# Second MoE's w_out by Strassen's algorithm, its output transposed, with the cosine's rounding on ScalarE and a pool for late weight conversions

## The chip, the cores and the metric

The kernel runs on one core of a Trainium2 chip. The metric is the device time of one execution, in microseconds (us). Times are medians of several runs, and beside them stands one execution taken by the hardware profiler. The engines are PE (TensorE, matrix products), DVE (VectorE), ACT (ScalarE), POOL (GpSimd) and SP (SyncE, which here only issues DMAs). PSUM holds matmul results in eight banks, SBUF the other tiles, DRAM the tensors.

## The reference

Block-causal attention (4 batches, 8 heads, 576 positions, head size 64) is followed by two mixtures on the 2304 tokens of 512 features. The change touches the second one alone.

```
def _moe_ref(x, w1, w2, w3, w_out):
    h = np.maximum(np.maximum(x @ w1, x @ w2), x @ w3)      # 512 -> 768
    return (h @ w_out).astype(np.float32)                   # 768 -> 512

def _moe2_ref(x, w_in, w_out):
    h = x @ w_in                                            # 512 -> 2048
    g = h * np.cos(h)
    return (g @ w_out).astype(np.float32)                   # 2048 -> 512
```

## The kernel before

**A recorded plan.** The program is not issued as it is written. Every operation is recorded with its dependencies (class `Plan`), priced by a table, and list-scheduled in several passes (`forward`, `backward`, `run`); the best order found is issued, in program order on each engine, with semaphores between engines. All instructions therefore carry line 214, and groups are told apart by tile names. `R.copy` and `R.scale` may go to ACT or DVE, as the plan chooses.

**Products in three parts.** A float32 product is made of three matmuls on operands split into a high and a low part (`split`: a rounding copy `hi`, then `lo = t - hi` on DVE): high x high, high x low, low x high.

**Stages.** Attention runs first, with matmuls of the first MoE put between its steps (`fill`, `units`). Weights arrive as 64-bit words and are converted on ACT and DVE (`whole`: two scalings, then three DVE operations), split, and kept in SBUF (first MoE) or stored to DRAM (`kept`, second MoE). `AHEAD` lists such conversions; eight of its eleven entries are called during attention (`ahead`, from the 17th item on), the others while the first MoE finishes. The first MoE leaves its result y, transposed, in DRAM in five parts (`y_dram`).

**Second MoE, first product.** The 2304 tokens make three superblocks of 768 (`NS`), each two halves of `TK` = 384 columns. In each there are eight steps j (`HALF`), and step j makes the rows j and j + 8 of h (128 features each) for both halves by Strassen's algorithm: seven products instead of eight on blocks of 256 x 128 and 256 x 384, each in two parts of K and three matmuls, that is 42 matmuls of 384 columns (`hstage`). The seven combinations of weights come ready from DRAM (`load_pair`: three tiles of 512 KB and one of 256 KB per step), those of y are made and split once per superblock (`split_y`, 14 operands). Three PSUM banks A, Bk, C collect the products, and DVE and ACT add them up into the tiles `ha`, `hu`, `hv`, `hh`.

**Cosine.** Each of the four tiles is scaled and rounded to an integer on DVE, reduced by 2 pi on DVE, put through Sin on ACT, multiplied on DVE and split into `gh` and `gl`. This is four times per step, on 384 columns.

**Second MoE, second product.** `ostage` of step j runs one step behind (`LAG`). Six PSUM banks hold 768 tokens x 512 features of the output; for each 128 tokens and each of the two rows of g, three matmuls with g as the stationary and w_out as the moving operand of 512 columns are added to the bank: 36 matmuls per step. After the eighth step the banks are copied to `osb` and stored. Half of w_out's tiles stay in SBUF, the others are loaded again; 13 of the 16 are converted in the second MoE's first superblock (`load_out`).

**Pools.** Pools open and close in the plan too: `wc`, where most tiles of the second MoE lie, opens when the first MoE's weights and work tiles are given up (`moe`, `wk`); `wb` opens when attention's pool closes.

Of the kernel before, what the change touches and what calls it, by code (L numbers as in the profile page):

```python
# [467 lines left out]
def fused_kernel(tc, qk, qk4, q1, k1, v2, w1, w2, w3, wout, w_in2, w_out2, out):  # L468
# [58 lines left out]
    def whole(src, pool, bufs):  # L527
# [4 lines left out]
        t = cv.tile([P, 512], F32, "t", tag="t", bufs=4)  # L532
# [371 lines left out]
    CVR = 2  # L904

# [14 lines left out]
    def pair_sums(j):  # L920

        x, y = (whole(w_in2[fc], cv, CVR) for fc in (j, j + HALF))
        a, b = (cv.tile([P, 512], F32, "t", tag="t", bufs=4) for _ in range(2))
        one, two = slice(0, QUARTER), slice(QUARTER, 2 * QUARTER)
        R.vector.tensor_tensor(a[:, one], y[:, one], y[:, two], ALU.add)
        R.vector.tensor_tensor(a[:, two], a[:, one], x[:, one], ALU.subtract)
        R.vector.tensor_tensor(b[:, one], x[:, one], y[:, one], ALU.subtract)
        R.vector.tensor_tensor(b[:, two], x[:, two], a[:, two], ALU.subtract)
        return x, a, b, y[:, two]

    def keep_pair(j):
        for n, t in enumerate(pair_sums(j)):
            both = cv.tile([P, 2, 512], F32R, "both", tag="raw", bufs=CVR)[:, :, :t.n]
            split(both[:, 0], both[:, 1], t)
            kept["in", j, n] = dram.tile([P, 2, t.n], F32, f"kept_in{j}_{n}")
            R.sync.dma_start(kept["in", j, n], f32(both))

    def keep_out(fc):
        both = cv.tile([P, 2, 512], F32R, "both", tag="raw", bufs=CVR)
        convert(w_out2[:, fc], both[:, 0], both[:, 1], cv, CVR)  # L940
        kept["out", fc] = dram.tile([P, 2, 512], F32, f"kept_out{fc}")
        R.sync.dma_start(kept["out", fc], f32(both))
# [5 lines left out]
    def ahead():  # L948
        if AHEAD and converted[0] == 4 * NFF:
            AHEAD.pop(0)()  # L950

# [30 lines left out]
    for n in range(NI + 1):  # L982
# [23 lines left out]
        if n > 16 and n % 3 and len(AHEAD) > 3:  # L1006
            ahead()
# [6 lines left out]
    wb = R.open(at, name="wb", bufs=1, side="right")  # L1014
    ps_o = R.open(ps_x, name="ps_o", bufs=1, space=PSUM, side="right")
    GROUPS = (512, 512, 512, QUARTER)

    def load_pair(n):

        where = {}  # L1020
        for x, w in enumerate(GROUPS):
            if n == 0 and x == 3:
                continue
            pool, bufs = (wc, 3) if x == 3 else (wb, 1) if n % 3 == 0 else (wc, 2)
            t = pool.tile([P, 2, w], F32R, f"pair{x}", tag=f"pair{x}", bufs=bufs)
            R.sync.dma_start(f32(t), kept["in", n % HALF, x])
            where[x] = t
        return where

    NY, FIXED = 18, 14  # L1030
    y_count = [0]

    def y_tile():
        slot = y_count[0] % NY
        y_count[0] += 1
        return (wb if slot < FIXED else wc).tile([P, 2, TK], F32R, f"y{slot}", tag=f"y{slot}")
# [5 lines left out]
    def split_y(s):  # L1042

        parts7 = [[y_tile() for k in range(2)] for _ in range(7)]
        for k in range(2):
            r = {}
            for i in range(2):
                for x in range(2):
                    r[i, x] = wb.tile([P, TK], F32, "yr", tag="yr", bufs=4)
                    load_y(r[i, x], k + 2 * i, 2 * TK * s + TK * x, TK)  # L1050
            a, b = (wb.tile([P, TK], F32, f"sum{i}", tag=f"sum{i}", bufs=1) for i in range(2))

            def put(n, t):
                split(parts7[n][k][:, 0], parts7[n][k][:, 1], t)

            sub = [ALU.subtract]
            put(0, r[0, 0])
            R.vector.tensor_tensor(a, r[0, 1], r[0, 0], *sub)
            R.vector.tensor_tensor(b, r[1, 1], a, *sub)
            put(1, b)  # L1060
            put(2, r[1, 0])
            R.vector.tensor_tensor(r[0, 1], r[1, 1], r[0, 1], *sub)
            put(3, r[0, 1])
            put(4, a)
            R.vector.tensor_tensor(r[1, 0], r[1, 0], b, *sub)
            put(5, r[1, 0])
            put(6, r[1, 1])
        return [[[parts7[n][k][:, i] for k in range(2)] for i in range(2)] for n in range(7)]

    ys = {0: split_y(0)}  # L1070
    pairs = {0: None}
    while AHEAD or fill:
        if AHEAD:
            ahead()
            if 0 in pairs and pairs[0] is None and ("in", 0, 3) in kept:
                pairs[0] = load_pair(0)
        for _ in range(2):
            if fill:
                fill.pop(0)[1]()
    R.close(wk)  # L1080
    R.close(moe, wk)

    wc = R.open(moe, name="wc", bufs=1)
    TWO_PI = 2.0 * math.pi
    woh, wol, g, banks = {}, {}, {}, {}

    def load_out(s, j):

        stays = j % 2 == 0
        if stays and s:  # L1090
            return
        for fc in (j, j + HALF):
            slot = f"out{fc}" if stays else f"out{j % 4}_{fc // HALF}"
            w = wc.tile([P, 2, 512], F32R, slot, tag=slot)
            if ("out", fc) in kept:
                R.sync.dma_start(f32(w), kept["out", fc])
            else:
# [156 lines left out]
```

## Time and profile before

| | us |
|---|---|
| median of 3 runs (846.71 to 847.55) | 846.73 |
| the profiled execution | 846.43 |
| its span, first to last instruction | 844.7 |
| PE busy | 835.3 (99%) |
| PE weight loads (beside matmuls) | 723.5 (86%) |
| DVE busy | 636.3 (75%) |
| ACT busy | 486.0 (58%) |
| POOL busy | 5.5 (1%) |

Busy time of an engine is the time in which at least one of its instructions ran. Matmuls are pipelined, so that each lasts longer than the distance from its start to the next one's start; what a matmul costs in a full stream is that distance. The same holds for DVE, whose instructions overlap a little. The stretches of the profile show the engines stage by stage, the chain of waits what ended last, the timelines single instructions. DMAs of all stages moved 155.15 MB, a mean of 184 GB/s.

### The profile page before, as it was taken

How to read it: one execution, taken by the hardware profiler on the slowest of the kernel's cores; microseconds unless marked ns; L12 is line 12 of the kernel's file. 1: busy time of each engine (PE TensorE's matmuls, PEld its weight loads, DVE VectorE, ACT ScalarE, POOL GpSimd, SP SyncE). 2: the span in 40 equal slices, each digit the busy share in tenths (PEclk: the TensorE clock that was granted, in tenths of full speed). 3: DMA queues.
4: the chain of work that ended last, by engine and by line, in shares of the span. 5: the costliest groups of instructions: out<-in, count | busy, mean ns of one | idle time of the engine just before them, and what ended most of it. 6: DMA issues, size and time to landing. Idle time of an engine off the chain costs nothing.

```text
span 844.7 us, 13582 instructions
## 1 busy us (share of the span) xinstructions
PE 835.3 (99%) x4722; PEld 723.5 (86%) x4722; DVE 636.3 (75%) x1441; ACT 486.0 (58%) x1114; POOL 5.5 (1%) x38
## 2 busy tenths in 40 slices
PE   8999999999999999999999999999999999999998
PEld 6787888888888888888899899899899899899896
DVE  7999999678877789536645899989746778757563
ACT  7998999658867678423333564645423445433333
POOL 2000000000000000000000000000000000000000
PEclk9999999999999999999999999999999999999999
DMA  8765665675566656442354857634866146935301
GB/s 287 224 191 158 205 203 178 193 222 177 179 210 220 193 185 224 142 149 106 131 167 153 343 177 245 234 137 149 310 230 215 48 152 209 335 105 185 100 1 75
DMA packets 68627, 155.15 MB, mean 184 GB/s; under 512 B 8528, under 2 KB 26960, under 8 KB 68560
## 3 DMA queue, kind: packets, MB, share of 16 engines
q1 hardware_dynamic: 68560, 154.30, 54.8%
q8 instruction: 37, 0.61, 0.3%
q14 instruction: 30, 0.25, 0.1%
HBM read 122.29 MB, written 31.98 MB: 183 GB/s over the span
## 4 chain that ended last, share of the span: by engine, by line
PE 95%; DVE 2%; ACT 2%; DMA 0%; issue 0%; POOL 0%; ACTq 0%; POOLq 0%
PE psm L214 56%; PE po L214 23%; PE tb L214 6%; PE X L214 4%; PE SB L214 3%; PE SA L214 3%; DVE top L214 1%; ACT other L214 0%; ACT prob L214 0%; DVE t L214 0%; DMA y<-hm 0%; ACT pt L214 0%; DVE pt L214 0%; DVE prob L214 0%; DVE other L214 0%
## 5 line engine op out<-in xcount | busy, mean ns | idle before, releaser
L214 PE MATMUL psm<-y,pair 128*128 128x384 f32 x1008 | 192.4, 337 | 1.6 <-ACT ha L214 1.4
L214 PEld LDWEIGHTS psm<-y,pair 128*128 128x128 f32 x1008 | 179.0, 188 | 10.7 <-ACT ha L214 1.8
L214 PE MATMUL po<-out,gh 128*128 128x512 f32 x576 | 178.5, 391 | 0.0
L214 PE MATMUL psm<-xhi,whi 128*128 128x512 f32 (+1 forms) x360 | 136.7, 380 | 0.7 <-ACT hm L214 0.7
L214 PE MATMUL psm<-xhi,wlo 128*128 128x512 f32 (+1 forms) x360 | 133.0, 370 | 0.0
L214 PE MATMUL psm<-xlo,whi 128*128 128x512 f32 (+1 forms) x360 | 132.9, 369 | 0.0
L214 PEld LDWEIGHTS po<-out,gh 128*128 128x128 f32 x576 | 106.9, 188 | 16.1
L214 PE MATMUL po<-out,gl 128*128 128x512 f32 x288 | 113.1, 393 | 0.0
L214 ACT ACTIVATE th<-th,halfpi 128x384 f32<-128x384 f32 x96 | 58.6, 617 | 72.4 <-DVE th L214 72.0
L214 PEld LDWEIGHTS psm<-xhi,wlo 128*128 128x128 f32 x360 | 67.9, 189 | 11.8
L214 PEld LDWEIGHTS psm<-xhi,whi 128*128 128x128 f32 x360 | 67.9, 189 | 9.6 <-ACT hm L214 1.0
L214 PEld LDWEIGHTS psm<-xlo,whi 128*128 128x128 f32 x360 | 68.1, 189 | 8.5
L214 DVE TENSOR_TENSOR hm<-psm,hm 128x512 f32<-128x512 f32 (+1 forms) x60 | 38.1, 635 | 47.8 <-PE psm L214 40.3
L214 ACT COPY pt<-tb 128x512 f32<-128x512 f32 (+2 forms) x100 | 58.4, 605 | 15.3 <-PE tb L214 15.0
L214 PEld LDWEIGHTS po<-out,gl 128*128 128x128 f32 x288 | 54.0, 187 | 11.5
L214 ACT CAST gh<-th 128x384 fp32r<-128x384 f32 x94 | 47.4, 510 | 27.6 <-DVE th L214 26.9
L214 DVE TENSOR_TENSOR hu<-psm,ha 128x384 f32<-128x384 f32 x24 | 13.4, 557 | 57.3 <-PE psm L214 47.8
L214 PE MATMUL tb<-ident,prob 128*128 128x128 f32 x374 | 54.7, 274 | 1.5 <-ACT pt L214 0.9
L214 PEld LDWEIGHTS tb<-ident,prob 128*128 128x128 f32 x374 | 45.0, 140 | 11.6 <-issue 2.2
L214 DVE TENSOR_TENSOR gl<-th,gh 128x384 fp32r<-128x384 f32 x96 | 51.9, 553 | 2.2 <-ACT gh L214 1.2
L214 ACT COPY hm<-psm 128x512 f32<-128x512 f32 (+1 forms) x48 | 26.0, 546 | 39.3 <-PE psm L214 33.4
L214 PE MATMUL psm<-hh,vhi 128*128 128x512 f32 (+1 forms) x120 | 46.0, 383 | 0.0
(152 smaller groups left out, 1448.3 us busy)
## 6 DMA issues: line engine op xcount, KB each, us to landing
pair<-kept_in SPq DMA_DIRECT2D x72, 512.0 KB, 5.3
kept_in<-both SPq DMA_DIRECT2D x24, 512.0 KB, 3.2
out<-kept_out SPq DMA_DIRECT2D x19, 512.0 KB, 6.2
raw<-w SPq DMA_DIRECT2D x18, 512.0 KB, 4.1
raw<-w_out SPq DMA_DIRECT2D x16, 512.0 KB, 3.6
raw<-w_in SPq DMA_DIRECT2D x16, 512.0 KB, 4.1
k<-k SPq DMA_DIRECT2D x24, 288.0 KB, 3.1
pair<-kept_in SPq DMA_DIRECT2D x24, 256.0 KB, 6.5
```

What stands on the lines that cost most here:

```text
L214: return lambda: getattr(real, method)(*[value(a) for a in args], **{k: value(a) for k, a in kw.items()})
```

## The change

**w_out by Strassen's algorithm.** The second product now takes the same form as the first, with the output transposed: w_out's combinations are stationary, and operands made of g are moving, 384 columns wide. Per superblock `ostage` runs once, behind all eight steps of `hstage`. It goes through the seven products in the order 1, 2, 6, 7, 4, 5, 3; for each and for each j it makes one operand of g (product 6 needs three differences of tiles of g first, product 7 one), splits it, and issues two units (d) of three matmuls. Four pairs of banks are used; products 1 and 2, 7 and 4, 5 and 3 add into the same bank, which is read in between. The output is written as (512, 2304); the transposition back happens outside of the kernel.

**Cosine.** The results of a step lie in one tile `g{j}` of four parts (h, v, a, u), and the chain runs on two parts at once, 768 columns: rounding on ACT, reduction on DVE, Sin on ACT, product on DVE, in place. There is no split here any more; `ostage` makes it.

**Conversions.** All 16 conversions of the second MoE go by pairs (`keep_pair`): eight of w_in, eight of w_out, each with four sums of 256 columns and four splits. Eight (w_in) are called in attention, five while the first MoE finishes, in a pool of their own (`cx`, with 6 raw and 12 spare tiles), three in the first superblock's steps.

**Buffers.** Weights of both products go through one ring of 14 slots of 512 KB (`w_tile`, 4 of them in `wb`), loaded in the order of use and reloaded for every superblock. Moving operands go through one ring of 22 (`operand`, 8 of them in `wb`), for y and for g. `bank8` takes the eight PSUM banks in turn.

```diff
-        t = cv.tile([P, 512], F32, "t", tag="t", bufs=4)
+        t = pool.tile([P, 512], F32, "t", tag="t", bufs=spare)
...
-    AHEAD = [lambda fc=fc: keep_out(fc) for fc in (9, 11, 13)]
-    for j in range(HALF):
-        AHEAD.insert(2 * j + 1 if j < 3 else len(AHEAD), lambda j=j: keep_pair(j))
+    AHEAD = [lambda *room, k=k, j=j: keep_pair(k, j, *room) for k in ("in", "out") for j in range(HALF)]
...
-        if n > 16 and n % 3 and len(AHEAD) > 3:
+        if n > 16 and n % 3 and len(AHEAD) > LEFT:
             ahead()
...
+    NW, NY, W_FIXED, Y_FIXED = 14, 22, 4, 8
...
+    def w_tile(shape):
+        slot = w_count[0] % NW
+        w_count[0] += 1
+        return (wb if slot < W_FIXED else wc).tile([P] + shape, F32R, f"w{slot}", tag=f"w{slot}")
...
+    ORDER = (1, 2, 6, 7, 4, 5, 3)
+    loads = []
+    for s in range(NS):
+        for j in range(HALF):
+            loads += [(s, "in", j, 0), (s, "in", j, 1)] + [(s, "last", j // 2)] * (j % 2 == 0) + [(s, "in", j, 2)]
+        loads += [(s, "out", n, q) for n in ORDER for q in range(HALF // 2)]
...
-        for f, x, t in ((j, 0, h), (j + HALF, 1, v), (j + HALF, 0, a), (j, 1, u)):
-            c = wc.tile([P, TK], F32, "th", tag="th", bufs=4)
...
-            R.vector.tensor_scalar(i32(c), t, 1.0 / TWO_PI, 0.25, ALU.mult, ALU.add)
+        for x in (0, 2):
+            t = both[:, x:x + 2].rearrange("p x t -> p (x t)")
+            c = wc.tile([P, 2 * TK], F32, "c", tag="c", bufs=2)
+            R.scalar.activation(i32(c), t, AF.Copy, scale=1.0 / TWO_PI, bias=0.25)
             R.vector.scalar_tensor_tensor(c, i32(c), -TWO_PI, t, ALU.mult, ALU.add)
             R.scalar.activation(c, c, AF.Sin, bias=halfpi)
-            R.vector.tensor_tensor(c, t, c, ALU.mult)
-            split(gh, gl, c)
-            g[s, f, x] = (gh, gl)
+            R.vector.tensor_tensor(t, t, c, ALU.mult)
+        g[j] = h, u, a, v
...
-    def ostage(s, j):
-        for x in range(2):
-            for t in range(TK // P):
...
-                for f in (j, j + HALF):
-                    gh, gl = g[s, f, x]
-                    with R.unit():
-                        for i, (a, w) in enumerate([(gh, woh[f]), (gh, wol[f]), (gl, woh[f])]):
-                            R.tensor.matmul(banks[n], a[:, ts], w, start=(f == 0 and i == 0),
-                                            stop=(f == NFC - 1 and i == 2))
...
+    def ostage(s):
...
+        for n in ORDER:
+            for j in range(HALF):
+                h, u, a, v = g[j]
+                if n == 6:
+                    R.vector.tensor_tensor(h, u, h, sub)
+                    t2 = wc.tile([P, TK], F32, "e", tag="e", bufs=4)
+                    R.vector.tensor_tensor(t2, v, h, sub)
+                    R.vector.tensor_tensor(a, a, t2, sub)
+                if n == 7:
+                    R.vector.tensor_tensor(u, v, u, sub)
+                y = operand()
+                split(y[:, 0], y[:, 1], {1: h, 2: a, 6: None, 7: u, 4: a, 5: h, 3: v}[n] or t2)
+                for d in range(2):
...
+                    three(ps[key], w, y, n in (1, 6, 7, 5) and j == 0, j == HALF - 1)
+                load_weights(len(loaded) + (j % 2))
...
+    for s in range(NS):
+        for j in range(HALF):
+            ahead()
+            load_weights(len(loaded) + 4)
             hstage(s, j)
...
+        ostage(s)
+        if s + 1 < NS:
+            ys[s + 1] = split_y(s + 1)
```

**How the order moves.** Three places follow, each of the kernel before and then of the changed one.

The first is DVE at the entry to the second MoE, of the kernel before, from the first step's first addition on. Here `hu`, `hv`, `ha`, `hh` are the step's sums, `th` the cosine's tile, `t`, `raw` and `out0`, `out8` belong to conversions of w_out.

```order
L214 TENSOR_TENSOR hu_5619<-psm_5585,ha_5608 128x384
L214 TENSOR_TENSOR out0_5612<-t_5357,out0_5612 128x512
L214 TENSOR_TENSOR out8_5621<-t_5510,out8_5621 128x512
L214 TENSOR_SCALAR th_5645<-hh_5636 128x384
L214 TENSOR_TENSOR hv_5653<-psm_5585,ha_5608 128x384
L214 SCALAR_TENSOR_TENSOR th_5645<-th_5645,hh_5636 128x384
L214 TENSOR_SCALAR t_5643<-t_5643 128x512
L214 TENSOR_TENSOR hv_5653<-psm_5647,hv_5653 128x384
```

In the changed kernel `g0` is the first step's tile, `hm` the first MoE's last output, `y8` to `y13` are operands of y whose tiles lie in `wc`, and `t`, `raw` belong to the one pair of w_out that is converted here.

```order
L214 COPY hm_5838<-psm_5784 128x256
L214 TENSOR_SCALAR t_5858<-raw_5793 128x512
L214 COPY g0_5860<-psm_5850 128x384
L214 TENSOR_SCALAR t_5858<-t_5858 128x512
L214 TENSOR_TENSOR g0_5860<-psm_5834,g0_5860 128x384
L214 SCALAR_TENSOR_TENSOR t_5858<-raw_5793,t_5858 128x512
L214 TENSOR_SCALAR t_5879<-raw_5816 128x512
L214 ISA t_5858<-raw_5793,t_5858 128x1024
L214 TENSOR_TENSOR y8_5877<-sum0_5582,y8_5877 128x384
L214 TENSOR_TENSOR y9_5889<-sum0_5678,y9_5889 128x384
L214 TENSOR_TENSOR y10_5894<-yr_5498,y10_5894 128x384
L214 TENSOR_TENSOR g0_5860<-psm_5834,g0_5860 128x384
```

The splits of y8 to y13 now stand between the evictions of the first step; before, all 14 were made ahead of it.

The second place is PE inside a step of the middle superblock of the kernel before; `pair` are w_in's weights, `po` the output banks.

```order
L214 MATMUL psm_7903<-y16_6386,pair1_7681 128x384 x3
L214 MATMUL psm_7903<-y17_6832,pair1_7681 128x384 x3
L214 MATMUL psm_7888<-y0_6690,pair0_7659 128x384 x3
L214 MATMUL psm_7888<-y1_6811,pair0_7659 128x384 x3
L214 MATMUL po_7046<-out6_6392,gh_7806 128x512 x2
L214 MATMUL po_7046<-out6_6392,gl_7815 128x512
L214 MATMUL psm_7903<-y2_6708,pair2_7716 128x384 x3
L214 MATMUL psm_7903<-y3_6835,pair2_7716 128x384 x3
```

The changed kernel's PE in the middle superblock's w_out: psm_7752 and psm_7761 are the banks of products 1 and 2, psm_7876 and psm_7885 those of 6, psm_7994 and psm_8000 those of 7, `w7` to `w13` weight slots.

```order
L214 MATMUL psm_7752<-y10_7818,w7_7683 128x384 x3
L214 MATMUL psm_7752<-y11_7896,w7_7683 128x384 x3
L214 MATMUL psm_7761<-y10_7818,w7_7683 128x384 x3
L214 MATMUL psm_7761<-y11_7896,w7_7683 128x384 x3
L214 MATMUL psm_7876<-y13_7881,w8_7675 128x384 x3
L214 MATMUL psm_7885<-y13_7881,w8_7675 128x384 x3
L214 MATMUL psm_7994<-y20_7812,w12_7759 128x384 x3
L214 MATMUL psm_8000<-y20_7812,w12_7759 128x384 x3
L214 MATMUL psm_7994<-y21_7839,w12_7759 128x384 x3
L214 MATMUL psm_8000<-y21_7839,w12_7759 128x384 x3
L214 MATMUL psm_7994<-y0_7847,w13_7795 128x384 x3
```

Matmuls of w_out no longer lie between those of w_in's steps; they follow each other, with products 6 and 7 interleaved.

The third place is DVE in a step of w_in, before at the end of the middle superblock's steps; `sum0`, `yr` and `y2`, `y4` belong to the next superblock's y.

```order
L214 TENSOR_SCALAR th_7937<-hh_7929 128x384
L214 SCALAR_TENSOR_TENSOR th_7937<-th_7937,hh_7929 128x384
L214 TENSOR_TENSOR hv_7950<-psm_7903,ha_7900 128x384
L214 TENSOR_TENSOR y2_7944<-yr_7759,y2_7944 128x384
L214 TENSOR_TENSOR th_7937<-hh_7929,th_7937 128x384
L214 TENSOR_TENSOR hv_7950<-psm_7946,hv_7950 128x384
L214 TENSOR_TENSOR y4_7958<-yr_7667,y4_7958 128x384
L214 TENSOR_TENSOR gl_7976<-th_7937,gh_7970 128x384
L214 TENSOR_TENSOR ha_7900<-psm_7903,ha_7900 128x384
L214 TENSOR_TENSOR sum0_7989<-yr_7931,yr_7785 128x384
```

The changed kernel's DVE in the middle superblock, around steps 4 and 5: `y0_7593` is an operand of w_out's product 1, and `g3_7386<-g3_7386` are differences that products 6 and 7 need.

```order
L214 TENSOR_TENSOR g5_7538<-psm_7529,g5_7538 128x384
L214 SCALAR_TENSOR_TENSOR c_7544<-c_7544,g4_7460 128x768
L214 TENSOR_TENSOR g4_7460<-psm_7456,g4_7460 128x384
L214 TENSOR_TENSOR g4_7460<-psm_7497,g4_7460 128x384
L214 TENSOR_TENSOR g3_7386<-g3_7386 128x384
L214 TENSOR_TENSOR g5_7538<-psm_7529,g5_7538 128x384
L214 TENSOR_TENSOR g4_7460<-g4_7460,c_7544 128x768
L214 SCALAR_TENSOR_TENSOR c_7576<-c_7576,g4_7460 128x768
L214 TENSOR_TENSOR g5_7538<-psm_7579,g5_7538 128x384
L214 TENSOR_TENSOR y0_7593<-g4_7460,y0_7593 128x384
L214 TENSOR_TENSOR g3_7386<-g3_7386 128x384
L214 TENSOR_TENSOR g4_7460<-g4_7460,c_7576 128x768
```

The rounding (TENSOR_SCALAR) and the split's subtraction (`gl`) have left the step; in their place stand differences and operands for w_out's products, made ahead of them.

## Rows read from the trace of the kernel before

**Rows 1.** The page of the profile, its first line.

```profile
span 844.7 us, 13582 instructions
```

**Rows 2.** Stretches: start:end, length, busy us (instructions) by engine, clock, DMA share, GB/s.

```profile
100.00:353.00 253.00, 253.00 (x1639) 210.56 (x1639) 211.04 (x468) 192.32 (x473) 0.00 (x0) 1.00 0.61 195
353.00:466.00 113.00, 112.78 (x641) 99.37 (x637) 54.11 (x110) 36.63 (x76) 0.00 (x0) 1.00 0.41 138
466.00:591.00 125.00, 123.57 (x623) 112.30 (x624) 116.00 (x250) 69.99 (x132) 0.00 (x0) 1.00 0.61 215
591.00:716.00 125.00, 125.00 (x625) 112.87 (x624) 86.90 (x189) 50.65 (x98) 0.00 (x0) 1.00 0.56 191
```

**Rows 3.** The chain of waits in order of time: start, us, what, count.

```profile
464.13 2.46 DMA y<-hm
...
475.03 2.10 PE psm L214 x12
...
638.32 6.16 PE po L214 x27
...
825.90 15.02 PE po L214 x66
```

**Rows 4.** Timeline of PE at the entry to the second MoE.

```profile
463.53 2.25 PE L214 MATMUL psm<-y,pair 128*128 128x384 f32 x12
467.22 5.59 PE L214 MATMUL psm<-y,pair 128*128 128x384 f32 x30 [1.43 <-ACT ha L214]
473.02 1.31 PE L214 MATMUL psm<-y,pair 128*128 128x384 f32 x6 [0.21 <-DVE ha L214]
```

**Rows 5.** Timelines of DVE: start, us, operation, output and inputs, shapes.

```profile
562.68 0.69 DVE L214 TENSOR_TENSOR out<-t,out 128x512 fp32r<-128x512 f32 x1
563.28 0.55 DVE L214 TENSOR_TENSOR th<-ha,th 128x384 f32<-128x384 f32 x1
...
640.20 0.55 DVE L214 SCALAR_TENSOR_TENSOR th<-th,hu 128x384 f32<-128x384 int32 x1
640.67 0.55 DVE L214 TENSOR_TENSOR th<-ha,th 128x384 f32<-128x384 f32 x1
...
653.88 0.35 DVE L214 TENSOR_SCALAR th<-ha 128x384 int32<-128x384 f32 x1
654.15 0.55 DVE L214 TENSOR_TENSOR hu<-psm,hu 128x384 f32<-128x384 f32 x1
```

**Rows 6.** Groups in 591 to 716 us: busy, mean ns, idle before, releaser.

```profile
L214 DVE TENSOR_TENSOR hu<-psm,ha 128x384 f32<-128x384 f32 x8 | 4.5, 558 | 23.4 <-PE psm L214 22.7 <-ACT y L214 0.7
...
L214 ACT CAST gh<-th 128x384 fp32r<-128x384 f32 x30 | 15.1, 510 | 7.2 <-DVE th L214 6.9
```

**Rows 7.** Timeline of ACT behind the entry.

```profile
468.68 0.47 ACT L214 COPY hh<-psm 128x384 f32<-128x384 f32 x1
...
469.74 1.28 ACT L214 ACT_TABLE_LOAD   x1
471.03 0.62 ACT L214 ACTIVATE th<-th,halfpi 128x384 f32<-128x384 f32 x1
...
483.31 0.67 ACT L214 ACTIVATE raw<-raw 128x512 int32<-128x512 uint32 x1
484.76 0.62 ACT L214 ACTIVATE th<-th,halfpi 128x384 f32<-128x384 f32 x1 [0.78 <-DVE th L214]
```

**Rows 8.** Stretches of the queue (last: DMA share, GB/s), and the page's DMA issues.

```profile
469.00:471.00 2.00, 1.00 0.96 379
...
473.00:475.00 2.00, 1.00 1.05 422
...
pair<-kept_in SPq DMA_DIRECT2D x72, 512.0 KB, 5.3
```

**Rows 9.** The output tile: duration min/median/max, first and last start.

```profile
L214 ACT COPY osb<-po x18: 565/587/593, 589.4 to 841.0; 128x512 f32<-128x512 f32 x18
L214 SPq DMA_DIRECT2D out<-osb x18: 332/338/424, 590.0 to 841.6; - x18
```

More of the change, by code (lines that the diff above doesn't have):

```diff
@@ L926, in pair_sums, with store @@
         R.vector.tensor_tensor(a[:, two], a[:, one], x[:, one], ALU.subtract)
[L927 to L932, printed above, removed]
+        R.vector.tensor_tensor(b[:, one], x[:, one], a21, ALU.subtract)
+        R.vector.tensor_tensor(b[:, two], a12, a[:, two], ALU.subtract)
+        def store(t, key, shape, part=None, cols=slice(None)):
+            if key not in kept:
+                kept[key] = dram.tile([P] + shape, F32, "kept_" + "_".join(map(str, key)))
+            to = kept[key] if part is None else kept[key][:, part]
+            R.sync.dma_start(to, f32(t[:, :, cols]))
@@ L944, in fused_kernel @@
-    AHEAD = [lambda fc=fc: keep_out(fc) for fc in (9, 11, 13)]
-    for j in range(HALF):
-        AHEAD.insert(2 * j + 1 if j < 3 else len(AHEAD), lambda j=j: keep_pair(j))
-    def ahead():
+            return both
+        pair = [2, 2, QUARTER]
+        if kind == "in":
+            for n, t in enumerate((x, a, b)):
+                store(parts(t), ("in", j, n), [2, 512])
+            store(parts(y[:, two]), ("last", j // 2), pair, j % 2)
+        else:
+            store(parts(x[:, one]), ("out", 1, j // 2), pair, j % 2)
+            for t, n, m in ((y, 2, 4), (a, 5, 6), (b, 7, 3)):
+                t = parts(t)
+                store(t, ("out", n, j // 2), pair, j % 2, one)
+                store(t, ("out", m, j // 2), pair, j % 2, two)
@@ L1042, in split_y @@
     def split_y(s):
[L1044 removed]
+        by = {n: [operand() for k in range(2)] for n in (1, 6, 2, 7, 5, 4, 3)}
         for k in range(2):
@@ L1083, in fused_kernel @@
     wc = R.open(moe, name="wc", bufs=1)
+    ys = {0: split_y(0)}
     TWO_PI = 2.0 * math.pi
[L1085 to L1097, printed above, removed]
-                convert(w_out2[:, fc], w[:, 0], w[:, 1], cv, CVR)
-                if not stays:
-                    kept["out", fc] = dram.tile([P, 2, 512], F32, f"kept_out{fc}")
-                    R.sync.dma_start(kept["out", fc], f32(w))
-            woh[fc], wol[fc] = w[:, 0], w[:, 1]
+    g = {}
@@ L1104, in hstage, with three @@
+    def three(ps, w, y, start, stop):
+        with R.unit():
+            for i, (u, v) in enumerate(((w[0], y[:, 0]), (w[0], y[:, 1]), (w[1], y[:, 0]))):
+                R.tensor.matmul(ps, u, v, start=start and i == 0, stop=stop and i == 2, skip_group_check=True)
     def hstage(s, j):
[L1106 to L1109 removed]
+        where = {1: (0, 0), 2: (0, 1), 5: (1, 0), 6: (1, 1), 7: (2, 0), 3: (2, 1)}
@@ L1122, in hstage @@
-        A, Bk, C = (bank()[:, :TK] for _ in range(3))
-        a, u, v, h = tile("ha"), tile("hu"), tile("hv"), tile("hh")
-        product(0, A, True)
+                if n == 4:
+                    w = [loaded[s, "last", j // 2][:, j % 2, i, k * P:k * P + P] for i in range(2)]
+                else:
+                    x, y = where[n]
+                    c0 = QUARTER * y + P * k
+                    w = [loaded[s, "in", j, x][:, i, c0:c0 + P] for i in range(2)]
+                three(ps, w, ys[s][n][k], start and k == 0, k == 1)
@@ L1125, in hstage @@
+        A, Bk, C = (bank8() for _ in range(3))
+        both = (wc if j else wb).tile([P, 4, TK], F32, f"g{j}", tag=f"g{j}")
+        h, v, a, u = (both[:, x] for x in range(4))
+        product(1, A, True)
         R.copy(a, A)
-        product(1, Bk, True)
+        product(6, Bk, True)
         R.vector.tensor_tensor(u, Bk, a, ALU.add)
```

187 lines of the change are left out of this document (89 added, 98 removed).

## The prediction

> **What bounds the kernel now.** I read the page's span first [rows 1], then the stretches by stage [rows 2]. The second MoE runs from 463.5 us to the end. In its middle stretch (591 to 716 us) TensorE (PE) is busy for all of 125.00 us, VectorE (DVE) for 86.90, ScalarE (ACT) for 50.65, and the granted clock is 1.00, the 2.4 GHz level, as in all stretches shown. A busy PE is not yet a full one, so the chain of waits comes next [rows 3]: in the second MoE it stays on PE, 12 matmuls of 384 columns in 2.10 us, 27 of 512 in 6.16. That is 0.175 and 0.228 us from start to start. The count closes it: 24 steps, each of 42 matmuls for w_in (7.35 us) and 36 for w_out (8.21), make 373.5 us, and the stretch from 463.53 to the end of the 66 matmuls at 840.92 [rows 3, 4] is 377.4. Of the 3.9 that are left, 1.6 are one stall at the entry (12 matmuls would end at 465.63): after 12 matmuls PE waits until 467.22 for an ACT copy [rows 4], which waited for the last y to reach DRAM [rows 3]. So the second MoE is PE work, end to end, and a matmul less is time less.
>
> **What the change removes: w_out's matmuls.** 864 matmuls of 512 columns go: 864 x 0.228 = 197.1 us. In their place come 3 superblocks x 7 products x 8 steps x 2 halves x 3 = 1008 of 384 columns, the shape that w_in's product already has: 1008 x 0.175 = 176.4. The gain on PE is 20.7 us, all of it on the path.
> By columns alone (7/8 of them left) it would be 23.0: each matmul pays 0.015 us beside its columns at either length (0.175 - 384 / 2.4 GHz, 0.228 - 512 / 2.4 GHz), and there are 144 more. The Trainium skill ("TensorE: Matmul & The Clock Gate", section on 56 against 53.3 ns) puts this fixed part at 2.5 ns; by it the gain would be an estimated 22.7 us. The rows here show 15 ns at both lengths, so the sum goes by 20.7.
>
> **What it adds on DVE.** The price first: ops of two inputs start 0.467 us apart at 384 elements and 0.60 at 512 [rows 5], 1.04 ns per element. A 768-wide one is not in the trace; it lies between 0.60 and two of 384 (0.93), and by the slope it is 0.87, which I take. Per superblock:
> - 8 steps of w_in: 5 evictions from PSUM (0.467 each) and 4 ops of 768: 8 x 5.8 = 46.4 us, beside 58.8 us of PE (336 x 0.175).
> - 56 operands of w_out, each a subtraction for its low part, 32 sums and differences ahead of them, 10 additions at the end: 98 x 0.467 = 45.8 us, beside another 58.8 of PE.
> - the next superblock's y: 14 splits and 8 differences, 10.3 us.
> Together 102.5 of 117.6 us, 87% (80 to 89% with the ends of the 768 price). Before it was 86.90 of 125, 70% [rows 2]. The first superblock also holds one pair of w_out conversions: two of 512 at full length (0.34 + 0.60 + 0.60 each), four sums of 256, four splits, some 6.5 us, making 93%.
> Does PE stay dense beside so full a DVE? Rows of before show it: in 466 to 591 us DVE is busy 116.00 of 125 (93%), and PE 123.57, with nothing lost but the entry stall [rows 2]. So I book nothing for the load as such, and keep the local shortage for the rivals. The cover of that zero is PE's lead: in the middle superblock DVE stood idle 23.4 us before the first eviction of a step alone, waiting for PE [rows 6].
>
> **ACT.** It takes the rounding (2 of 768 per step) and 56 casts. A cast of 384 takes 0.51 us [rows 6], a copy out of PSUM 0.47, a Sin of 384 0.62 [rows 7]; 768-wide ones lie between 0.62 and 1.24. Per superblock at most 8 x (2 x 0.47 + 4 x 1.24) + 70 x 0.51 = 83 of 117.6 us, so ACT doesn't bind. Copy-type and Sin activations already alternate after one table load of 1.28 us [rows 7], so none is added.
> The Trainium skill ("ScalarE: Activation LUTs", Rules for kernel authors) speaks against this move: products and sums belong on VectorE. The rows say what that would do here: DVE's rounding of 384 steps 0.27 us [rows 5], so 16 more of 768 (0.27 to 0.54 each) would lift DVE from 102.5 to 107 to 111 us per superblock. The trace goes against the rule in this place, since DVE is the fuller engine; by it the first rival below would be likelier than I make it.
>
> **Transfers.** Weights now come afresh for both products: 56 tiles of 512 KB per superblock, 88 MB in all, some 99 MB with y, out and the last conversions, over 353 us: 280 GB/s. In the entry's burst the queue moved 379 to 422 GB/s for sixteen microseconds, and a 512 KB load landed in 5.3 us [rows 8]; 14 slots are 13 loads of lead, each standing for 2.1 us of PE: 27 us. Hidden. SP's issue of 0.34 us [rows 9], about 220 times, is 75 of 353 us. Each load waits on SP until PE has read its slot; behind it stand the output stores and y loads, which have that lead too.
>
> **Entry and handovers.** The order of DVE at the entry puts six operand splits (y8 to y13, in the pool that opens only when the last y is in DRAM) between the evictions. PE can run 24 matmuls (4.2 us) without them; the last y landed at 466.59 [rows 3], 3.1 us after PE's start there, so the first split would be done 1.1 us later (0.51 + 0.56), at 4.2 us too. The second step's weights are issued after 466.59 too and land some 5.3 us later [rows 8], at 471.9, the second tile 1.3 us behind (512 KB at 400 GB/s); PE would want them at 470.9. So the stall is 0 to 2.5 us where before had 1.6: -1.6 to +0.9, I take 0. In w_out three handovers per superblock read a bank that the next product adds to: nine, each 0 to 0.56 us (one eviction [rows 6]), so 0 to 5.0. In w_in's product of before there are three such in each of 24 steps, and all gaps beside the entry's are the 2.3 us left above, 0.03 each; I take 2.0 for the nine, nearer to that row, but above it, since nothing else stands between and DVE is fuller.
>
> **Conversions, attention, end.** Eight pairs of w_in go into attention in place of five pairs and three singles: some 13 us more of DVE in 100 to 353 us, where it is busy 211 of 253 (83%); that makes 89%, under the 93% shown. Five pairs of w_out and two of the last three fall in 353 to 466 us, where DVE has 54 of 113 busy [rows 2]; PE works off the first MoE there without a gap. Nothing booked. The end is one op and a store (0.59 us, 256 KB) [rows 9], and becomes one DVE addition and 192 KB: the same.
>
> **The sum.** The profiled execution took 846.43 us, its span 844.7 and 1.73 around it; the median of the runs shown is 846.73. 846.4 - 20.7 + 0 + 2.0 = **827.7 us**.
>
> **Rivals.**
> First, DVE is short in one place: product 6. Per step it asks for three differences and a split, 4 x 0.467 = 1.87 us, while PE uses the operand up in 6 x 0.175 = 1.05. With nothing made ahead this costs 8 x 0.82 = 6.5 us per superblock, 19.6 in all: 847, no change. For it: the temporary e has four buffers, shared with the output tiles, so only half can be made ahead. Against: the order makes differences and splits during w_in's steps, and puts product 7 and part of 4 and 5 among product 6's. Half of the price gives 837.
> Second, slower: the split's round trip through ACT does not overlap. Then each operand of product 6 takes 0.467 x 3 + 0.51 + 0.55 = 2.46 us against 1.05, and the other six products 1.06 against 1.05: 8 x 1.41 = 11.3 per superblock and 34 in all, 861.5. It decides from a loss of 6.9 us per superblock on. Against: casts and subtractions of before run side by side for different tiles, DVE at one per 0.467 [rows 5].
> Third, attention's added 13 us of DVE come half onto the path: 834.
> Fourth, the change doesn't do what it says: the transfers fall back to the 215 GB/s of 466 to 591 us [rows 2]. 99 MB would then take 460 us, 107 more. That rate was demand, not a ceiling, by rows 8.
>
> **How the numbers follow.** Forecast, 822.5 to 832: 0.66. First rival in part (832 to 842) 0.17, in full (no change) 0.03; attention 0.06; second rival 0.06, transfers 0.02. The range is 822.5 (entry at its best, no handover cost, and 1.6 us gained in attention by its other order) to 840, which leaves out under 0.2. Within 0.2% is what a measurement of this kernel can tell from no change: 1.7 us. Faster 0.89, same 0.03, slower 0.08.
>
> **What would show it.** Right: 2016 matmuls of 384 columns at 0.175 us, a second MoE of 354 to 358 us with PE busy throughout, DVE near 87% of its last two superblocks, one table load before the first Sin. First rival: PE idle before w_out's matmuls, released by DVE's y subtractions, once per superblock. Second: the same released by ACT casts, with DVE idle on ACT. Attention: the first w_in matmul later than 465 us. Transfers: PE released by loads of w. What would make me wrong is a start-to-start above 0.175 in w_out.

## The result and the profile after

The changed kernel takes 821.93 us (median; 820.99 to 822.11), the kernel before 846.72 beside it: ratio 0.9703 (95% interval 0.9686 to 0.9720), 24.8 us faster. The forecast was 827.7, a gain of 19.0; the time lies 0.6 us under the forecast's range.

The page of the profile after, first line and PE's and DVE's busy time; [rows 1] answers to the first.

```profile
span 819.2 us, 14203 instructions
...
PE 810.7 (99%) x4866; PEld 734.1 (90%) x4866; DVE 703.3 (86%) x1491; ACT 547.3 (67%) x1200; POOL 5.5 (1%) x38
```

Its chain of waits (start, us, what, count), and PE's timeline at the entry to the second MoE [rows 3, 4].

```profile
355.20 110.34 PE psm L214 x624
...
471.88 73.08 PE psm L214 x420
...
552.65 263.26 PE psm L214 x1517
...
815.93 0.56 DVE du L214
```

```profile
463.28 2.25 PE L214 MATMUL psm<-y,w 128*128 128x384 f32 x12
466.18 2.55 PE L214 MATMUL psm<-y,w 128*128 128x384 f32 x13 [0.65 <-DVE g L214]
468.98 1.13 PE L214 MATMUL psm<-y,w 128*128 128x384 f32 x5 [0.25 <-DVE y L214]
470.43 1.30 PE L214 MATMUL psm<-y,w 128*128 128x384 f32 x6 [0.32 <-issue]
471.88 80.53 PE L214 MATMUL psm<-y,w 128*128 128x384 f32 x463 [0.15 <-DVE g L214]
552.65 263.24 PE L214 MATMUL psm<-y,w 128*128 128x384 f32 x1517 [0.24 <-DVE y L214]
```

The second MoE starts at 463.28 (before: 463.53), so attention and the first MoE take as long as before, with other conversions among them. It ends at 815.91: 352.6 us where before took 377.4. From 552.65 us on PE runs 1517 matmuls without a pause, each 263.26 / 1517 = 0.1735 us behind the one before it. The pauses at the entry and at 552 us make 1.6 us (0.65 + 0.25 + 0.32 + 0.15, and 0.24 ahead of 552.65), the same as before.

The three superblocks (columns as in [rows 2]):

```profile
463.00:580.00 117.00, 115.38 (x661) 113.84 (x659) 113.69 (x216) 73.96 (x133) 0.00 (x0) 1.00 0.88 315
580.00:698.00 118.00, 118.00 (x682) 118.00 (x682) 104.19 (x192) 68.62 (x122) 0.00 (x0) 1.00 0.81 279
698.00:816.00 118.00, 117.90 (x681) 117.58 (x679) 94.47 (x172) 61.15 (x107) 0.00 (x0) 1.00 0.65 224
```

DVE (the third busy time) is busy for 97, 88 and 80% of them, and still PE waits for it only in the first. The last number is the rate of transfers in GB/s.

### The profile page after: what moved, and what is told of

It is laid out like the page before. It is cut to its first block, busy times and chain, and to the rows that moved or that the text cites. A ratio compares the mean times of both kernels' runs of the same rounds, so it can differ in the third digit from the quotient of the medians.

```text
span 819.2 us, 14203 instructions
## 1 busy us (share of the span) xinstructions
PE 810.7 (99%) x4866; PEld 734.1 (90%) x4866; DVE 703.3 (86%) x1491; ACT 547.3 (67%) x1200; POOL 5.5 (1%) x38
## 4 chain that ended last, share of the span: by engine, by line
PE 94%; DVE 3%; ACT 2%; DMA 1%; issue 0%; SPq 0%; ACTq 0%
PE psm L214 78%; PE tb L214 7%; PE X L214 4%; PE SA L214 3%; PE SB L214 3%; ACT prob L214 1%; DVE y L214 1%; DMA knat<-qk 1%; DMA qnat<-qk 0%; DVE g L214 0%; DVE t L214 0%; ACT pt L214 0%; ACT other L214 0%; DVE e L214 0%; DVE other L214 0%
## 5 line engine op out<-in xcount | busy, mean ns | idle before, releaser
L214 PE MATMUL psm<-y,w 128*128 128x384 f32 x2016 | 351.0, 334 | 1.6 <-DVE g L214 0.8
L214 PEld LDWEIGHTS psm<-y,w 128*128 128x128 f32 x2016 | 349.3, 188 | 3.2 <-DVE y L214 1.1
L214 ACT CAST y<-g 128x384 fp32r<-128x384 f32 x143 | 69.3, 511 | 32.8 <-PE psm L214 19.3
L214 DVE TENSOR_TENSOR y<-g,y 128x384 fp32r<-128x384 f32 x144 | 74.3, 548 | 0.0
L214 DVE TENSOR_TENSOR g<-psm,g 128x384 f32<-128x384 f32 x120 | 64.2, 549 | 7.7 <-PE psm L214 7.1
L214 ACT ACTIVATE c<-c,halfpi 128x768 f32<-128x768 f32 x48 | 45.1, 940 | 28.9 <-DVE c L214 28.9
L214 DVE TENSOR_TENSOR hm<-psm,hm 128x512 f32<-128x512 f32 (+1 forms) x60 | 37.9, 632 | 16.1 <-PE psm L214 12.2
L214 DVE SCALAR_TENSOR_TENSOR c<-c,g 128x768 f32<-128x768 int32 x48 | 45.5, 947 | 2.0 <-ACT c L214 1.9
L214 DVE TENSOR_TENSOR g<-g,c 128x768 f32<-128x768 f32 x48 | 45.3, 948 | 0.4
L214 ACT ACTIVATE prob<-prob,sums 128x448 f32<-128x448 f32 (+7 forms) x76 | 41.9, 619 | 5.5 <-DVE sums L214 5.4
L214 PE MATMUL psm<-hh,vlo 128*128 128x512 f32 (+1 forms) x120 | 44.3, 370 | 0.0
```

The source lines that it names most:

```text
L214: return lambda: getattr(real, method)(*[value(a) for a in args], **{k: value(a) for k, a in kw.items()})
```

## Where the missing 5.8 us were: the price of a matmul

The forecast took its prices from pieces of before that lie between two changes of product: 12 matmuls in 2.10 us, 27 in 6.16 [rows 3]. PE's timeline of before, one step of the middle superblock closer:

```profile
595.40 0.61 PE L214 MATMUL po<-out,gh 128*128 128x512 f32 x2
...
596.08 0.61 PE L214 MATMUL po<-out,gh 128*128 128x512 f32 x2
...
597.44 1.23 PE L214 MATMUL psm<-y,pair 128*128 128x384 f32 x6
598.51 0.63 PE L214 MATMUL po<-out,gh 128*128 128x512 f32 x2
...
599.21 2.26 PE L214 MATMUL psm<-y,pair 128*128 128x384 f32 x12
601.31 0.63 PE L214 MATMUL po<-out,gh 128*128 128x512 f32 x2
...
606.91 0.63 PE L214 MATMUL po<-out,gh 128*128 128x512 f32 x2
...
607.61 0.62 PE L214 MATMUL po<-out,gh 128*128 128x512 f32 x2
...
608.30 0.62 PE L214 MATMUL po<-out,gh 128*128 128x512 f32 x2
...
608.99 0.62 PE L214 MATMUL po<-out,gh 128*128 128x512 f32 x2
...
609.67 0.62 PE L214 MATMUL po<-out,gh 128*128 128x512 f32 x2
...
613.07 1.23 PE L214 MATMUL psm<-y,pair 128*128 128x384 f32 x6
```

Deep in a piece of 512 columns three matmuls take 596.08 - 595.40 = 0.68 us, 0.2267 each. Six of 384 behind it take 1.07 where 6 x 0.1735 = 1.04; the next three of 512 take 0.70. A step of the middle superblock is 15.63 us long (597.44 to 613.07), and 42 x 0.1735 + 36 x 0.2267 = 15.45. So 0.18 us lie at this step's eight changes between the products, 0.0225 each; PE's order has 185 such changes in the 24 steps. I call the price without them the clean price. With clean prices the second MoE adds up so ("booked" is the forecast's figure):

| us | before | after | difference | booked |
|---|---|---|---|---|
| matmuls | 1008 x 0.1735 + 864 x 0.2267 = 370.8 | 2016 x 0.1735 = 349.8 | -21.0 | -20.7 |
| pauses of PE | 1.6 | 1.6 | 0 | 0 |
| what is left | 5.0 | 1.2 | -3.8 | +2.0 |
| whole | 377.4 | 352.6 | -24.8 | -18.7 |

Of the 5.0 us that are left in before, 185 x 0.0225 = 4.2 would be the changes. The other 0.8, and the 1.2 after, lie beside the pauses: 463.28 + 12 x 0.1735 is 465.36, and the next matmul starts at 466.18, 0.82 later, where 0.65 are shown as idle.

**One width for both products.** The kernel before, with w_out's matmuls cut to 384 columns, so that a quarter of the output's columns is left out:

```diff
-R.tensor.matmul(banks[n], a[:, ts], w, ...)
+R.tensor.matmul(banks[n][:, :TK], a[:, ts], w[:, :TK], ...)
```

> The kernel before with w_out's matmuls cut from 512 to 384 columns (a quarter of the output's columns is left out). Question: why the same 384-column matmul cost 0.175 us between w_out's pieces of 512 columns and 0.1735 us in the changed kernel's unbroken stream. In the trace of before a step of the middle superblock takes 15.63 us (597.44 to 613.07), while 42 x 0.1735 + 36 x 0.2268 = 15.45; 0.18 us are left over for some 8 to 10 changes between the two products. Theory (a change of the column count costs about 0.02 us): a step of the middle superblock takes 78 x 0.1735 = 13.53 us, though PE still goes back and forth between the products 203 times. Rival (going from one product to the other costs, whatever the columns): 13.71 us. The whole: 846.7 - (185 x 0.020 by the theory, 0 by the rival) - 864 x (0.2268 - 0.1735) = 797 or 801 us, plus what DVE adds in the first superblock, where its 116 us of work meet a PE time of 108 us: up to 8 us.

Measured: 797.55 us. Its chain of waits, two steps of the middle superblock:

```profile
618.15 4.68 PE po L214 x27
631.67 4.68 PE po L214 x27
```

A step takes 13.52 us, 78 x 0.1733, with 203 changes of product in the order: the loss is gone when the widths are equal. The rival (a change of product costs, whatever the columns) would have needed 13.71.

**Widths mixed inside the changed kernel.** If a change of width as such cost 0.0225 us, it should come back here. Four doses, whose code cuts follow: the second matmul of each unit at 320 columns (64 columns of that correction are left out); the first at 512 (`ps512` gives the whole bank, and the extra columns go to its unused end); w_in's products as blocks of four wide and two narrow; one wide matmul in every fourth unit, told as a change to the second dose.

```diff
-R.tensor.matmul(ps, u, v, ...)
+m = 320 if i == 1 else TK
+R.tensor.matmul(ps[:, :m], u, v[:, :m], ...)
```

```diff
-R.tensor.matmul(ps, u, v, ...)
+wide = i == 0
+R.tensor.matmul(ps512(ps) if wide else ps, u, y.rearrange("p i t -> p (i t)")[:, :512] if wide else v, ...)
```

```diff
-wide = i == 0
+wide = i == 0 and turn[0] % 4 == 0
```

For the blocks the six matmuls of a product of w_in make one unit, wide ones first:

```diff
+with R.unit():
+    for i in range(6):
+        (w, y), wide = both[i // 2 if i < 4 else i - 4], i < 4
...
```

> The changed kernel with the second of the three matmuls of every unit of the second MoE cut from 384 to 320 columns (the last 64 columns of that correction are left out). Each unit now changes the column count twice: about 1344 changes in 2016 matmuls. By columns alone a 320-column matmul is 64/2.4 = 27 ns shorter, so that 672 of them save 17.9 us. Theory (each change costs about 0.02 us): 1344 x 0.02 = 27 us come back, 821.9 - 17.9 + 27 = 831 us, and superblocks two and three take about 236.0 - 11.9 + 17.9 = 242 us together. Rival (changes cost nothing; 0.175 in before was something else): PE needs 224 us for superblocks two and three and the whole is 804 us, plus up to 5 us in the first superblock, where DVE's 114 us of work do not shrink: 804 to 809.

> The changed kernel with the first of the three matmuls of every unit of the second MoE widened from 384 to 512 columns (128 columns more are computed into the unused end of the bank; the result stays). The kernel then changes between 512 and 384 columns some 1344 times in 2016 matmuls, where before did so 185 times. By columns alone 672 x 128/2.4 ns = 35.8 us: 821.9 + 35.8 = 857.7 us. Theory (every change between 384 and 512 costs 0.02 us, as the 0.18 us left over per step of before, with about 9 changes, said): 857.7 + 1344 x 0.02 = 885 us. Rival (a change costs 0.004 us, as with 384 and 320): 863 us. Second rival (nothing per change; before lost its 0.18 us per step only in the first units after a long block of the other width): 857 to 859 us. PE is the bound in all of them, since DVE's 104 us meet 130 us per superblock.

> The changed kernel with w_in's products in blocks: of the six matmuls of a product four are widened to 512 columns and stand first, two of 384 follow (the extra columns go to the unused end of the bank); w_out's stay at 384. This makes 672 wide matmuls, as many as the alternating kernel had, but 335 changes of width in place of 1343. By columns alone 821.9 + 35.8 = 857.7 us. Question: before lost 0.0225 us per change (0.178 us a step, 7.7 changes), the kernel that changed at every unit only 0.0067 (8.9 us over 1343). Theory (a change costs a settling time that alternation cuts short, so that it costs more between longer blocks): 0.015 to 0.0225 us per change, 863 to 865 us. Rival (0.0067 for every change): 860 us. Second rival (the loss goes with the number of wide matmuls, not with changes): 8.9 us again, 866.6 us.

> The changed kernel with the first matmul of every fourth unit alone widened to 512 columns: 168 wide matmuls, each between some 11 of 384, 336 changes of width. By columns alone 821.9 + 168 x 0.0533 = 830.9 us. Theory (a change costs more where blocks are longer, as in before, whose blocks of 384 had 6 to 12 matmuls): 0.015 to 0.0225 per change, 836 to 838.5 us. Rival (0.0067 for every change): 833.1 us. Second rival (loss by the number of wide matmuls, 8.9 us for 672): 833.1 us as well; the kernel with blocks tells these two apart.

Measured: 811.24, 866.62, 860.18 and 832.80 us. These kernels start the second MoE 1.6 to 3.1 us later than the changed one (the plan lays out attention anew), so I read the longest unbroken stream of PE from each chain of waits, in this order:

```profile
474.88 168.31 PE psm L214 x1008
```

```profile
471.50 389.83 PE psm L214 x1992
```

```profile
472.56 382.54 PE psm L214 x1986
```

```profile
473.23 354.47 PE psm L214 x1980
```

| kernel | stream, us | at clean prices | over | changes of width in it | us each |
|---|---|---|---|---|---|
| 384 and 320 | 168.31 | 672 x 0.1735 + 336 x 0.1468 = 165.9 | 2.4 | 672 | 0.004 |
| 512 and 384 | 389.83 | 664 x 0.2267 + 1328 x 0.1735 = 380.9 | 8.9 | 1328 | 0.007 |
| blocks | 382.54 | 652 x 0.2267 + 1334 x 0.1735 = 379.3 | 3.3 | 325 | 0.010 |
| every fourth unit | 354.47 | 166 x 0.2267 + 1814 x 0.1735 = 352.4 | 2.1 | 332 | 0.006 |

(0.1468 is an estimate: 0.1735 less 64 columns at 2.4 GHz.) My theory of a fixed 0.0225 us per change falls: in these streams a change costs 0.004 to 0.010. A loss by the number of wide matmuls falls too, since 652 and 664 of them lose 3.3 and 8.9. The settling theory falls in the form put on record, 0.015 and more in the last two. Shown is: before's loss needs unequal widths (none without), and it has no fixed price per change.

What sets the price stays open, but the lengths of the pieces have a part in it. In before the loss lies on the first matmuls behind a change: in the piece of 27 above, the sets of three start 0.70, 0.69, 0.69 and then 0.68 us apart, so that entering it costs some 0.04 us, where entering a piece of three costs 0.02 (598.51 to 599.21). The doses never repeat before's pieces: three of them go wide for one matmul at a time or narrow for one, and the blocks go back to 512 after two matmuls of 384. That the change of product counts, nothing here shows. In the kernel with 512 and 384, 658 of the stream's 663 distances from one wide matmul to the next are 0.586 or 0.587 us in the trace, although in w_in's steps at least every second unit starts another product. That is read from one trace; no run put before's pieces inside one product.

## The parts undone

**Cosine's rounding back on DVE**, in the changed kernel, and **the rounding alone on ACT**, in the kernel before. The cut is of the first; in the second the same line changes the other way:

```diff
-R.scalar.activation(i32(c), t, AF.Copy, scale=1.0 / TWO_PI, bias=0.25)
+R.vector.tensor_scalar(i32(c), t, 1.0 / TWO_PI, 0.25, ALU.mult, ALU.add)
```

> The changed kernel with one part undone: cosine's rounding back on DVE, 16 instructions of 768 columns per superblock. In before the 384-column rounding took 0.27 us step to step; 768 columns are put at 0.47 us, so that DVE gets 7.5 us per superblock: 113.7 + 7.5 = 121 of 117 us in the first, 104 + 7.5 = 112 of 118 in the second, 94.5 + 7.5 = 102 of 118 in the third. Theory (DVE costs time only where its work exceeds PE's): the first superblock grows by 4 to 7 us, the other two by nothing: 826 to 829 us. Rival (the rounding's place is free, as the planner moves other DVE work out of the way): within 1 us of 821.9. Second rival (a DVE at 95% already holds PE up): the second superblock grows by 2 us or more as well, 829 to 833.

> The kernel before with one part of the change alone: cosine's rounding on ScalarE, on 384 columns. DVE loses 32 x 0.27 = 8.6 us per superblock. In before PE was dense in the first superblock with DVE at 93% (466 to 591 us: PE 123.57, DVE 116.00 of 125) and in the second with DVE at 70%, so the theory (DVE did not set the end of before) expects 846.7 within 0.5 us. Rival (DVE at 93% already cost something in before's first superblock, the 1.4 us that PE idled there): 845.3.

Measured: 825.90 and 846.12 us (ratio to before 0.9743, and 0.9988, interval 0.9979 to 0.9998). PE's timeline and the first two superblocks with the rounding on DVE, and PE at the entry of the kernel before with the rounding on ACT:

```profile
465.78 4.75 PE L214 MATMUL psm<-y,w 128*128 128x384 f32 x25
...
546.85 15.24 PE L214 MATMUL psm<-y,w 128*128 128x384 f32 x83 [0.84 <-DVE y L214]
562.31 116.78 PE L214 MATMUL psm<-y,w 128*128 128x384 f32 x672 [0.22 <-DVE dv L214]
679.65 141.81 PE L214 MATMUL psm<-y,w 128*128 128x384 f32 x816 [0.55 <-DVE dv L214]
```

```profile
463.00:580.00 117.00, 114.56 (x655) 111.66 (x654) 113.53 (x216) 62.69 (x118) 0.00 (x0) 1.00 0.85 317
580.00:698.00 118.00, 117.45 (x678) 117.13 (x677) 112.75 (x213) 57.08 (x108) 0.00 (x0) 1.00 0.80 274
```

```profile
466.85 5.87 PE L214 MATMUL psm<-y,pair 128*128 128x384 f32 x30 [0.66 <-ACT ha L214]
```

The second MoE takes 355.7 us (465.78 to 821.5) in place of 352.6: 3.1 lost, most of them ahead of 562 us, 0.55 in a pause at 679. The other 2.5 us of the longer span are a later start. So the theory's place was right and its 4 to 7 us too much: DVE still shows 113.53 us in the first stretch, and what it can't do there slides into the second, which goes from 104.19 to 112.75 us; a DVE at 96% costs 0.55 us there. So the rounding's move is worth 3 us of the second MoE here. In before it is worth 0.9 us (0.2 to 1.8 by the interval), between the two expectations, and the entry's pause is shorter, 0.66 us in place of 1.43. The Trainium skill ("ScalarE: Activation LUTs", Rules for kernel authors) sends products and sums to VectorE; in this kernel the measurement goes against it.

**The pool for late conversions.** Without it; with it, but small; and with all conversions in it:

```diff
-ahead(cx, 6, 12)
+ahead()
```

```diff
-ahead(cx, 6, 12)
+ahead(cx, 2, 4)
```

```diff
-LEFT, REST_AHEAD, PACE = 8, 3, 4
+LEFT, REST_AHEAD, PACE = 8, 0, 4
```

> The changed kernel with one part undone: the five conversions that are called while the first MoE finishes use the old ring of 2 raw and 4 spare tiles instead of the pool of their own with 6 and 12. Theory (the pool lets them run ahead, two buffers make each pair wait for its predecessor's stores): part of the conversions slides into the first superblock, where DVE is 97% busy (113.7 of 117 us); at some 5 us of DVE work for a pair, one to two pairs late cost 2 to 8 us: 824 to 830 us. Rival (110 us of the first MoE are time enough for two buffers too): 821.9 within 1 us, up to 3 us either way from the planner's other order in attention, which is read from the start of the second MoE (463.3 us in the changed kernel).

> The changed kernel with its pool for late conversions kept, but with 2 raw and 4 spare tiles in it instead of 6 and 12: the size of the shared ring, without sharing it. Without the pool the kernel took 841.9 us: PE idled 9.0 us in the first MoE (7.36 us of it at 443.65 behind a cast whose x load stood behind conversions' stores), ran at half clock behind that, and had been 36 matmuls (8 us) further back at 353 us. Theory (the number of buffers does it): most of it comes back, 832 to 842 us, with a pause of 3 us or more in front of xhi in the first MoE. Rival (sharing the ring with the first MoE's own conversions does it): 822 to 826 us.

> The changed kernel with all eight remaining conversions called while the first MoE finishes, none in the first superblock. Theory (DVE's 97% in the first superblock cause the pauses of PE at its entry and at 552 us, 0.65 + 0.25 + 0.32 + 0.15 + 0.24 = 1.6 us, and some hidden in the stream): the second MoE takes 351 us in place of 352.6, the whole 820 to 821 us. Rival (the three conversions stand ahead of the first cosine on DVE anyway, so nothing is taken from the superblock; the splits of y make the pauses): 352.6 us for the second MoE, 821.9 us. Third (DVE at 81 of 110 us in the first MoE gets too full): the second MoE starts 1 us or more after 463.3 us.

Measured: 841.88, 834.13 and 821.67 us. I had priced the pool's loss at 2 to 8 us of DVE work; it is 20, and elsewhere. Without the pool PE idles in the first MoE, and its granted clock falls (PE's timeline; the chain of waits, 441 to 446 us; stretches as in [rows 2], the clock third from the end):

```profile
443.65 0.58 PE L214 MATMUL psm<-xhi,whi 128*128 128x256 f32 x1 [7.36 <-ACT xhi L214]
...
446.42 0.58 PE L214 MATMUL psm<-xhi,whi 128*128 128x256 f32 x1 [0.88 <-ACT xhi L214]
```

```profile
441.11 0.15 DVE both L214
...
441.71 0.43 DVE t L214
...
442.80 3.14 DMA t<-x
```

```profile
436.00:446.00 10.00, 2.18 (x8) 1.43 (x6) 5.18 (x11) 4.29 (x9) 0.00 (x0) 0.74 0.49 159
446.00:448.00 2.00, 1.58 (x6) 1.33 (x7) 1.33 (x3) 0.78 (x2) 0.00 (x0) 0.50 1.06 331
...
452.00:454.00 2.00, 2.00 (x19) 2.00 (x18) 0.83 (x3) 0.65 (x2) 0.00 (x0) 1.00 0.97 274
```

The cast `xhi` waits for the load of x into a tile `t`, and the chain leads from that load back to the conversions' DVE work on `both` and `t`: `t` is the ring of four that the conversions use too. The second MoE starts at 483.56, 20.3 us late. Of these, 8.9 are idle PE: the two pauses shown and 0.62 us at 373. Some 4.1 go with the 1.2 GHz level: beside the second pause, the 26 matmuls from 443.65 to 451.73 take 7.2 us, and 26 x 0.12 would be 3.1. The other 7.3 stand ahead of the pauses: by 353 us 36 matmuls of 512 columns (8.2 us) less of the first MoE were done, though attention itself was further on. With the small pool the first MoE runs without that pause, but the conversions end later, and `wb`, which takes the pool's place, opens later. PE's timeline and SP's of that kernel, and SP's of the changed one:

```profile
473.80 2.26 PE L214 MATMUL psm<-y,w 128*128 128x384 f32 x6 [6.67 <-DVE y L214]
```

```profile
468.40 0.45 SPq L214 DMA_DIRECT2D w<-kept_in  x1
```

```profile
444.67 0.97 SPq L214 DMA_DIRECT2D w<-kept_in  x2
```

The second MoE's first weights are asked for at 468.40 in place of 444.67, and PE stands 6.67 us before its first operand of y, which lies in `wb` too. The second MoE starts 10.5 us late (473.80); the 3.8 us beside the pause lie in attention and the first MoE. So the total (832 to 842 expected) held and the place that I named, `xhi`, did not. Both properties count: an own ring spares x's loads, a large one opens `wb` in time. Calling all conversions early changes nothing (821.67, the rival's time): between 467 and 521 us DVE's work falls from 53.60 to 49.13 us, and the pauses stay at the entry (0.52 and 1.67 us, for `hm` and y on ACT).

## The handovers and product 6

Two parts of the forecast were not seen at all in the profile after: the nine handovers, and product 6 short of DVE. To see what hides them, the eight banks are parted, four for each product, and in another kernel the four tiles `e` become two:

```diff
-slot = b_count[0] % 8
+slot = first + b_count[first // 4] % 4
...
-ps[key] = bank8()
+ps[key] = bank8(4)
```

```diff
-wc.tile([P, TK], F32, "e", tag="e", bufs=4)
+wc.tile([P, TK], F32, "e", tag="e", bufs=2)
```

> The changed kernel with the eight PSUM banks parted: four in turn for w_in's steps, four in turn for w_out's products, instead of one ring of eight. Question: why the nine handovers of w_out's banks (the read of one product before the next adds to the same bank) cost nothing, where 2.0 us were booked. Theory (PE has units of another product's banks to run meanwhile, because eight banks are in turn): with four, the third bank pair of a superblock (product 7) must wait until product 2 has been copied out; an eviction takes 0.55 us and the copy 0.47 us, so that pauses of 0.5 to 1.0 us at three or four places per superblock give 4 to 12 us: 826 to 834 us. Rival (two pairs are enough, since one pair is filled while the other is read): within 1.5 us of 821.9, and no pause above 0.3 us in the stream of superblocks two and three.

> The changed kernel with two instead of four tiles e, which hold product 6's difference on its way to its split, and the results of products 2 and 4 on their way to the output. The forecast's first rival was that product 6 runs short of DVE (three differences and a split, 2.8 us of ACT and DVE work per j for 1.04 us of PE work) unless its operands are made ahead; four tiles let them be made ahead. Theory (the lead over product 6 comes from the operand ring of 22 and from h and a being changed in place, not from e): 821.9 within 1.5 us apart from attention's order (the start of the second MoE). Rival (e is the lead): at the eight operands of product 6 DVE and ACT work of 1 to 2 us each is no longer ahead, 8 to 13 us per superblock less what product 7 hides: 830 us or more, with PE waiting for y from e.

Measured: 822.08 us with banks parted (second MoE 352.2 us), 825.88 with two `e` (356.9 us). PE's timeline with parted banks, and the chain of waits with two `e`:

```profile
470.87 2.18 PE L214 MATMUL psm<-y,w 128*128 128x384 f32 x11 [0.76 <-DVE y L214]
473.31 344.21 PE L214 MATMUL psm<-y,w 128*128 128x384 f32 x1980 [0.25 <-DVE g L214]
```

```profile
547.15 0.56 DVE y L214
547.71 0.47 DVE e L214
...
558.64 3.75 DVE y L214 x8
...
563.84 104.32 PE psm L214 x600
...
798.46 23.17 PE psm L214 x132
```

Two bank pairs are enough for no further pause in 1980 matmuls: one pair is filled while the other is read. My theory of 4 to 12 us falls. With two `e` the chain lies on DVE's y, e and g for 17 us at product 6 of the first superblock (547 to 563) and again of the third (781 to 798): the forecast's first rival, but PE has other units meanwhile and the second MoE loses 4.2 us, not 8 or more. Four tiles hide it; both of my numbers for this run were off.

No version here that computes the whole result beats the changed kernel by more than the runs scatter: PE is busy for 810.7 of its 819.2 us.

## Why the forecast came out as it did

- **What bounds it, and the main term: right.** PE bound the second MoE before and binds it after. 1008 matmuls for 864 was booked at a gain of 20.7, by clean prices it is 21.0.
- **The price of 0.175 and 0.228: the step that failed.** It was read from pieces with a change at each end, so that the changes' cost sat in the matmul's price and was carried over to a stream that has none: 2016 x 0.0015 = 3.0 us too much. The 2.3 us that these prices left over in before stayed in the sum as well, and after the change only 1.2 were found: 1.1 too much. "Each matmul pays 0.015 us" is 0.0135 at 384 columns and 0.0134 at 512 (0.1735 - 384 / 2.4 GHz, 0.2267 - 512 / 2.4 GHz). The Trainium skill ("TensorE: Matmul & The Clock Gate", section on 56 against 53.3 ns) gives 2.5 ns, at 128 and at 512 columns. The rows here do not agree, at 384 and 512.
- **The handovers: mis-sized, 2.0 where nothing was paid.** The 0.03 us each that the forecast gave w_in's handovers were nearer, but by luck: the 2.3 us that they were read from lay at the changes of width and beside the pauses. The three terms make 6.1 us; 5.8 of them show in the median.
- **The range's low end: too high.** Of the price's error nothing was taken into the range, and the second MoE's 352.6 us lie under the 354 to 358 named as a sign; 3.0 us more at the low end would have held the time.
- **DVE's load: right.** 87% forecast, 88% in the middle superblock; 93% forecast and 97% found in the first. That it costs nothing while PE has a lead held; the kernel with the rounding on DVE shows where that ends.
- **ACT (68.6 us in the middle superblock, at most 83 forecast), transfers (279 GB/s there, 280 forecast as a mean), entry (no change), attention and end (463.28 us): right.** For the late conversions the forecast booked nothing, because DVE had room there; it is the pool that holds them off the path, and without it they cost 20 us.

## What to carry over

Take the price of an instruction from a stream like the one that will run, and if only mixed pieces are there, sum a whole period and see what is left: the remainder belongs to the changes, and goes with them. That remainder is not a fixed price per change: it was 0.0225 us in before's pieces and 0.004 to 0.010 in the doses. A tile ring shared between a background job and a stage's loads cost 7.8 us here (841.88 against 834.13), and an own one that is too small 12.2 (834.13 against 821.93), since loads waited for the ring or for the pool behind it, and PE for the loads.

## What was not expected of the hardware

A change between 512 and 384 columns cost some 0.0225 us in before, 0.006 to 0.010 in the changed kernel with its shorter pieces, and a change of product at equal widths none. After the 7.36 us pause PE's granted clock stood at 0.50 (1.2 GHz) and was back at 1.00 in the stretch from 452 us; matmuls of 256 columns were 0.21 us apart at the lower level and 0.12 from 452 us on.
